# Two row blocks written ahead of their logits, and other warm-up matmuls on TensorE

## The chip, the cores and the metric

The kernel runs on one core of a Trainium2 chip. The metric is the device time of one execution in microseconds (us); the time of a kernel is the median of its runs. TensorE (PE) does matmuls and transposes, VectorE (DVE), ScalarE (ACT) and GpSimd (POOL) do element-wise work, SyncE (SP) issues most DMAs, POOL the indirect ones.

## The reference

Three layers follow one another: attention over 768 positions with a local window and pooled keys, a mixture of 8 experts with a skip score on its output, and a dense layer with a cosine gate.

```python
def _attn_ref(q, k, v):                      # (2, 8, 768, 64)
    k_sum = k.reshape(B, H, nb, 32, D).max(axis=3)
    v_sum = v.reshape(B, H, nb, 32, D).mean(axis=3)
    ...
    a = softmax(concatenate([scores_l_m, scores_s]))
    return a @ concatenate([v, v_sum])

def _moe_ref(x, w_skip, w_gate, w1, w2):     # x (1536, 512)
    do_compute = x @ w_skip > 0
    xc = x[do_compute]
    e_idx = argmax(xc @ w_gate)
    gate_w = softmax(xc @ w_gate)[e_idx]
    for e in range(8):
        h = maximum(xc[e_idx == e] @ w1[e], 0)
        y[e_idx == e] = gate_w * (h @ w2[e])
    out[do_compute] = xc + y

def _moe2_ref(x, w_in, w_out):               # w_in (512, 2048)
    h = x @ w_in
    return (h * cos(h)) @ w_out
```

## The kernel before

The 1536 rows of `x` are 12 blocks of 128. Attention runs as a software pipeline of 24 steps; two steps make one block. A block leaves attention turned (`xT[n]`, features on partitions). `logits` multiplies it with the skip and gate weights (`pl`, eight matmuls in two groups for two blocks, one of four for one), and copies the product out (`ls`). `turn_rows` turns the block back with four transposes into `pk`, from which ACT copies `xtok`, and `write_rows` lets SP write that to `xb` in memory. `st_q` and `st_sum`, together `st_l`, turn the logits (`pq`) and add them up into `LG`. `route1` finds the expert of each row (`R`), `route2` counts places, and `slots` multiplies one-hot matrices (`OR`) with `R` into `pia`, `pib` and `pic`, from which DVE makes the row numbers for the gathers (`GIA` for the first). Blocks 0 to 9 pass through that within the pipeline; blocks 10 and 11 come at its end, and the routing behind them.

POOL gathers the rows of expert 0 and 1 from `xb` by GIA into `xg`; the first needs every row write. When they are there, PE turns them (`ptx`, line 601), multiplies them with the first weights of the expert (`ph`, line 639), then does the second half of `slots` (line 575), the next `ptx` and the next expert. POOL goes on with the gathers of all other experts (`xg`, `xo`, `xm`). Then come the experts, and the dense layer (`pf` line 1219, `py` line 1398) to the end.

Engines run their instructions in the order of the code, each its own queue; the code is that order, with no scheduler behind it. Weights come in pieces from a list: `load_piece(after, lag)` lets SP issue the next piece, behind a given instruction where one is given, else at an ordinary pace.

`warm` (line 166) issues matmuls of zeros whose results nobody reads: 512 columns wide, or narrow with 64. They stand at the beginning (while the first keys load), in attention step 3, between the parts of the routing (`W1_`, `W2_`, `W3_` = 3, 3, 4, all wide) and behind the routing (`WN` = 7 wide and 56 narrow), while the first gather is under way.

```python
W1_, W2_, W3_, WN = 3, 3, 4, 7
```

Of the kernel before, what the change touches and what calls it, by code (L numbers as in the profile page):

```python
# [19 lines left out]
P = 128  # L20
# [10 lines left out]
NT = NTOK // P  # L31
# [9 lines left out]
W1_, W2_, W3_, WN = 3, 3, 4, 7  # L41
# [78 lines left out]
def tile_kernel(ctx: ExitStack, tc: tile.TileContext, consts, qh, kh, vh, vw, w9, w1, w2, w_in, w_out, out):  # L120
    nc = tc.nc
# [8 lines left out]
    xb = dpool.tile([NTOK + 1, DM], F32, name="xb")  # L130
# [34 lines left out]
    def warm(pool, tag, n, w=512):  # L165

        t = pool.tile([P, w], F32, tag=tag, name="warm")
        for _ in range(n):
            nc.tensor.matmul(t, wz[:, 0:P], wz[:, 0:w], start=True, stop=True)
# [8 lines left out]
    def load_w(u):  # L178
        pool = ring[u % NU]
        wt[u] = pool.tile([P, 4096], F32, tag="w", name="w")  # L180
        for part in range(4):
            wq.append((u, part))

    def load_piece(after=None, half=None):

        if not wq:
            return
        u, part = wq.pop(0) if half != 0 else wq[0]
        e, kind = divmod(u, 2)
        k, w = (4, w1) if kind == 0 else (8, w2)  # L190
        ks, fs = slice(part * k // 4, (part + 1) * k // 4), slice(None)
        if half is not None and kind == 0:
            fs = slice(512 * half, 512 * half + 512)
        elif half is not None:
            ks = slice(2 * part + half, 2 * part + half + 1)
        d = nc.sync.dma_start(out=wt[u].rearrange("p (k f) -> p k f", k=k)[:, ks, fs],
                              in_=w[e].rearrange("(k p) f -> p k f", p=P)[:, ks, fs])
        if after is None and len(pieces) >= ahead_of[-1]:
            after = pieces[-ahead_of[-1]]
        if after is not None:  # L200
            tc.add_manual_dep(d.ins, after.ins.name, SYNC, reason="pace")
        pieces.append(d)
# [8 lines left out]
    ps_s = at.enter_context(tc.tile_pool(name="ps_s", bufs=2, space=PSUM))  # L211
    ps_t = at.enter_context(tc.tile_pool(name="ps_t", bufs=2, space=PSUM))
    ps_x = at.enter_context(tc.tile_pool(name="ps_x", bufs=1, space=PSUM))
    ps_m = at.enter_context(tc.tile_pool(name="ps_m", bufs=3, space=PSUM))
# [85 lines left out]
    def kend(b):  # L300
        nc.gpsimd.tensor_copy(out=kT[b][:, :, SK - QT:SK], in_=kT[b][:, :, 0:QT])
# [38 lines left out]
    def st_norm(i, fill=None):  # L340
        sm, su = sc[i]
        nc.vector.tensor_scalar(out=su, in0=su, scalar1=1e-9, scalar2=None, op0=ALU.add)
        if fill is not None:
            fill()
        nc.vector.reciprocal(out=su, in_=su)  # L345
        nc.gpsimd.tensor_tensor(out=sm, in0=sm, in1=su.unsqueeze(2).to_broadcast([P, NP, P]), op=ALU.mult)  # L346
# [30 lines left out]
    xT = {}  # L377
# [36 lines left out]
    rows = {}  # L414
    IOB = ap_.tile([P, NS], BF16, name="IOB")

    def logits(n, eng):

        s = xT[n]
        pl = ps_m.tile([P, P], F32, tag="m", name="pl")  # L420
        for p in range(NP):
            nc.tensor.matmul(pl[32 * p:32 * p + 32, :], w9s[:, p, :], s[:, p, :], start=True, stop=True,
                             skip_group_check=True)
        ls = a2.tile([P, P], F32, tag="ls", name="ls")
        eng(out=ls, in_=pl)
        xT[n] = ls
        return s

    def turn_rows(n, s, pool, tag):
        pk = pool.tile([P, NP, P], F32, tag=tag, name="pk")  # L430
        for p in range(NP):
            nc.tensor.transpose(pk[:, p, :], s[:, p, :], ident)
        rows[n] = a3.tile([P, DM], F32, tag="xtok", name="xtok")
        nc.scalar.copy(out=rows[n], in_=pk.rearrange("p n a -> p (n a)"))

    def write_rows(n):
        nc.sync.dma_start(out=xb[n * P:(n + 1) * P, :], in_=rows.pop(n))

    def st_x(n):
        turn_rows(n, logits(n, nc.vector.tensor_copy), ps_m, "m")  # L440
# [74 lines left out]
    def one_hot(ns, a, b):  # L515
        for n in ns:
            nc.vector.tensor_scalar(out=OR[:, n, a:b], in0=IOB[:, a:b], scalar1=RK[:, n:n + 1],
                                    scalar2=None, op0=ALU.is_equal)
# [156 lines left out]
    kput(0, slice(0, NP), 1, 6, nc.scalar.copy)  # L675
    for u in range(4):
        load_w(u)
    warm(ps_t, "t", 27)
    warm(ps_t, "t", 12, 64)
    for i in range(NI - 1):  # L680
        fill, hot = (), None
        if i >= 8 and i % 2 == 0:
            fill, hot = route1_parts((i - 8) // 2)
        if i >= 10 and i % 2 == 0:
            fill = (lambda f=fill[0], n=(i - 10) // 2: (one_hot((n,), 0, NS), f()),) + fill[1:]
        if i != 4:
            st_scores(i, fill)
        if i == 6:
            kend(0)
        if i == 5:  # L690
            nc.gpsimd.tensor_copy(out=IOB, in_=cst[:, C_IOTA:C_IOTA + NS])
            nc.vector.tensor_copy(out=ub, in_=cst[:, C_U:C_U + P])
            nc.vector.tensor_copy(out=G5[:, :, 0:1], in_=cst[:, C_TT:C_TT + NT].unsqueeze(2))
            nc.vector.tensor_copy(out=G5[:, :, 1:2], in_=cst[:, C_P:C_P + 1].unsqueeze(1).to_broadcast([P, NT, 1]))
        if i >= 1:
            st_norm(i - 1, hot)
        if hot is not None:
            route2_ids((i - 8) // 2)
        if i == 3:
            warm(ps_x, "x", 6)  # L700
        if i >= 3:
            st_T(i - 3)
        if i in (3, 4):
            for j in (range(3), range(3, 6))[i - 3]:
                vmean_mm(0, j)
            if i == 4:
                vmean_copy(0)
                st_scores(i)
        st_exp(i)
        if i in (4, 14):  # L710
            vmean_spread(i // 14)
        if i >= 4:
            st_pv(i - 4)
        if i in (12, 13):
            for j in (range(4), range(4, 6))[i - 12]:
                vmean_mm(1, j)
        if i >= 9 and i % 2 == 1:
            route2_parts((i - 9) // 2)()
        if i >= 6 and i % 2 == 0:
            st_x((i - 6) // 2)  # L720
        if i >= 7 and i % 2 == 1:
            st_q((i - 7) // 2)
        if i in KS:
            kpool(1, KS.index(i))
        if i == 9:
            kpool_out(1, slice(0, NP))
            kput(1, slice(0, NP), 0, 6, nc.vector.tensor_copy)
            kend(1)
        if i == 13:
            vmean_copy(1)  # L730
        if i == NQ + 3:
            early.close()
            lists = ctx.enter_context(tc.tile_pool(name="lists", bufs=1, side="right"))
            GIA, SIA, GIB, SIB, GIS, SIS = (lists.tile([n, NE], U32, name=m) for n, m in (
                (QA, "GIA"), (QA, "SIA"), (P, "GIB"), (P, "SIB"), (YT, "GIS"), (YT, "SIS")))
            GTA, GTB, GTS, SEL = (lists.tile([n, NE], F32, name=m) for n, m in ((QA, "GTA"), (P, "GTB"), (YT, "GTS"), (P, "SEL")))
            wpb = ctx.enter_context(tc.tile_pool(name="wpb", bufs=2, side="right"))
            ring[4] = ring[5] = wpb
            load_w(4)
            load_w(5)  # L740
        if i == 7:
            nc.sync.dma_start(out=xb[NTOK:NTOK + 1, :], in_=wz.bitcast(F32)[0:2, :])
        if PC(i) and i % 2:
            load_piece()
        for _ in range(MORE.get(i, 0)):
            load_piece()
        if i % 4 == 2 and (i + 6) // 2 < NI // 2:
            load_q((i + 6) // 2)
        if i >= 7 and i % 2 == 1:
            write_rows((i - 7) // 2)  # L750

        if i >= 4 and i % 2 == 0 and i != NQ + 2:
            load_v(i - 1)
        if i == NQ:
            load_v(NQ + 1)
        if i % 2 == 0:
            window(i)
        if 2 <= i <= 5:
            load_k(1, i - 2)
        if 5 <= i <= 10:  # L760
            load_vn(1, i - 5)
        if PC(i) and i % 2 == 0:
            load_piece()
# [25 lines left out]
    route2((NT - 4,))  # L789
    last_pv(L)  # L790
    st_l(NT - 3)
    rows11 = logits(NT - 1, nc.vector.tensor_copy)
    rows10 = logits(NT - 2, nc.scalar.copy)
    route1((NT - 3,))
    turn_rows(NT - 1, rows11, ps_x, "x")
    write_rows(NT - 1)
    st_l(NT - 1)
    st_l(NT - 2)
    turn_rows(NT - 2, rows10, ps_m, "m")
    write_rows(NT - 2)  # L800
    load_piece()
    pia = ps_t.tile([QA, 6, NE], F32, tag="t", name="pia")
    pib = ps_t.tile([P, 6, NE], F32, tag="t", name="pib")
    pic = ps_x.tile([YT, 6, NE], F32, tag="x", name="pic")
# [44 lines left out]
    warm(ps_s, "s", W3_)  # L849
    slots(pib, lb, tail)  # L850
    slots(pic, lc, tail)
    warm(ps_s, "s", WN)
    warm(ps_s, "s", 56, 64)
    slot_ids(pib, idb)
    load_piece(slot_gi(idb, False, GIB), 1)
    slot_ids(pic, idc)
# [458 lines left out]
    for e in range(NE):  # L1315
# [18 lines left out]
        if e == 4:  # L1334
            cv_alloc(0, 0)
            t = wpa.tile([P, 2, 4, 512], F32R, tag="w", name="yb")
# [4 lines left out]
        if e == 6:  # L1341
            t = wpb.tile([P, 4096], F32, tag="w", name="y4")
# [188 lines left out]
```

## Time and profile before

| | us |
|---|---|
| median of 3 runs | 479.47 |
| lowest and highest | 478.92, 479.60 |
| the profiled execution | 479.16 |
| its span, first to last instruction | 477.2 |
| PE, PEld, DVE, ACT, POOL busy | 437.9, 319.6, 301.2, 214.2, 142.5 |

PEld is PE's loading of weights, which overlaps its matmuls. Busy shares are over the whole span, while the stages have different limits; so the table by stage and the timeline are to be read with them. "Issue" is time in which an engine waited for nothing that the profile shows, "remote" a wait for a signal whose sender the profile doesn't name. In the timeline a row is a group of like instructions that follow one another: start, length, engine, line, what it writes and reads, count, and in brackets how long the engine was idle before and what ended that.

### The profile page before, as it was taken

The numbers are of one execution on the slowest core, as the hardware profiler recorded it, in microseconds if no ns is written. First come the engines' busy times: TensorE is split into PE (matmuls) and PEld (weight loads), VectorE is DVE, ScalarE is ACT, GpSimd is POOL, SyncE is SP. The second block draws the span as 40 slices with busy tenths as digits, with TensorE's granted clock in tenths as the row PEclk, the third lists the DMA queues.
The fourth block names the chain that finished last, engine by engine and source line by source line (L and its number), as shares of the span: only waits on it lengthen the run. The fifth ranks groups of instructions, "written<-read, shape, count | busy, mean of one in ns | idle before, by whom it ended". The sixth has DMA issues, their size and how long they took to land.

```text
span 477.2 us, 9227 instructions
## 1 busy us (share of the span) xinstructions
PE 437.9 (92%) x3273; PEld 319.6 (67%) x3276; DVE 301.2 (63%) x842; ACT 214.2 (45%) x523; POOL 142.5 (30%) x170
## 2 busy tenths in 40 slices
PE   8899999509989897999999999999999999999994
PEld 4667676304444343567888888888888888888883
DVE  5697897106040051567679797998989956472831
ACT  2988993001332123346567566473646415051600
POOL 0755762650120024454053222231222100003043
PEclk9999999857999999999999999999999999999999
DMA  8999998799958389324312232321322000002021
GB/s 265 322 310 330 346 302 277 233 279 365 384 178 337 131 311 396 90 73 128 117 40 93 89 102 80 129 88 46 100 78 88 0 1 0 1 1 88 2 110 66
DMA packets 35180, 76.05 MB, mean 159 GB/s; under 512 B 4185, under 2 KB 10843, under 8 KB 35124
## 3 DMA queue, kind: packets, MB, share of 16 engines
q1 hardware_dynamic: 31876, 66.07, 42.2%
q0 software_dynamic: 3248, 9.27, 6.1%
q8 instruction: 31, 0.51, 0.5%
q14 instruction: 25, 0.20, 0.1%
HBM read 68.15 MB, written 7.60 MB: 159 GB/s over the span
## 4 chain that ended last, share of the span: by engine, by line
PE 29%; issue 18%; DVE 3%; POOL 3%; POOLq 0%; ACT 0%; DVEq 0%; ACTq 0%
PE pf L1219 14%; PE py L1398 11%; PE py L1464 2%; POOL out L627 2%; DVE g L1235 1%; PE pt L1144 1%; POOL wx L938 1%; DVE cvu L929 0%; DVE cvc L930 0%; DVE u L1225 0%; DVE c L1229 0%; POOLq L1527 0%; DVE nn L1224 0%; DVE cvu L927 0%; ACT u L1223 0%
## 5 line engine op out<-in xcount | busy, mean ns | idle before, releaser
L1219 PE MATMUL pf<-yb,wx 128*128 128x512 f32 x576 | 133.9, 390 | 1.3 <-DVE xg L1006 0.8
L1219 PEld LDWEIGHTS pf<-yb,wx 128*128 128x128 f32 x576 | 107.7, 188 | 24.2 <-PEq L1199 1.3
L1398 PE MATMUL py<-wx,g 128*128 128x512 f32 (+1 forms) x540 | 121.6, 384 | 0.0
L1398 PEld LDWEIGHTS py<-wx,g 128*128 128x128 f32 x540 | 99.9, 188 | 20.2
L1223 ACT ACTIVATE u<-pf,qbias 128x512 f32<-128x512 f32 x44 | 30.1, 685 | 78.2 <-PE pf L1219 78.0
L938 POOL TENSOR_TENSOR wx<-cvc,wx 128x512 fp32r<-128x512 f32 x24 | 34.7, 1446 | 94.7 <-ACT wx L937 91.5
L1404 DVE TENSOR_TENSOR ya<-py,ya 128x512 f32<-128x512 f32 (+1 forms) x37 | 23.8, 672 | 28.2 <-PE py L1398 26.2
L1235 DVE TENSOR_TENSOR g<-c,g 128x512 fp32r<-128x512 f32 x40 | 41.3, 1032 | 0.1
L336 ACT ACTIVATE sm<-sm,nm 128x128 f32<-128x128 f32 x96 | 37.4, 393 | 2.1 <-DVE nm L324 2.0
L1228 ACT ACTIVATE c<-u 128x512 f32<-128x512 f32 x44 | 27.6, 627 | 16.0 <-DVE g L1235 16.0
L627 POOL DMA_INDIRECT out<-ya,PERM x11 | 10.9, 992 | 79.9 <-DVE ya L1404 79.2
L1224 DVE TENSOR_SCALAR nn<-u 128x512 f32<-128x512 f32 x44 | 18.6, 424 | 23.1 <-ACT u L1223 23.0
L1225 DVE TENSOR_TENSOR u<-u,nn 128x512 f32<-128x512 f32 x44 | 30.5, 693 | 1.5
L1229 DVE TENSOR_TENSOR c<-pf,c 128x512 f32<-128x512 f32 x44 | 30.1, 684 | 0.7 <-ACT c L1228 0.7
L346 POOL TENSOR_TENSOR sm<-sm,su 128x512 f32<-128x512 f32 x23 | 24.2, 1050 | 21.3 <-DVE su L345 10.8
L324 DVE CUSTOM_DVE_ANT_0 sm<-sc,cst 128x128 f32<-128x128 f32 x96 | 23.6, 284 | 7.0 <-PE sc L317 6.0
L1234 ACT CAST g<-c 128x512 fp32r<-128x512 f32 x44 | 26.7, 607 | 0.2 <-DVE c L1229 0.2
L937 ACT CAST wx<-cvc 128x512 fp32r<-128x512 f32 x24 | 14.9, 622 | 16.1 <-DVE cvc L930 16.1
L1083 DVE SCALAR_TENSOR_TENSOR xm<-pox,GTB,xm 128x512 f32<-128x512 f32 x2 | 1.5, 750 | 30.4 <-PE pox L1073 30.4
L627 POOL DMA_INDIRECT xb<-xg,SIA x8 | 7.8, 978 | 41.9 <-DVEq L1199 15.5
L317 PE MATMUL sc<-kT,q 64*64 64x128 f32 x384 | 17.5, 282 | 2.3 <-DVE nm L324 1.4
L929 DVE SCALAR_TENSOR_TENSOR cvu<-cvc,cvu 128x512 int32<-128x512 int32 x24 | 17.5, 731 | 3.0 <-DVE cvu L927 0.5
(256 smaller groups left out, 631.5 us busy)
## 6 DMA issues: line engine op xcount, KB each, us to landing
w<-w SPq DMA_DIRECT2D x62, 512.0 KB
raw<-w_in SPq DMA_DIRECT2D x16, 512.0 KB
raw<-w_out SPq DMA_DIRECT2D x16, 512.0 KB
kT<-kh SPq DMA_DIRECT2D x8, 384.0 KB
vn<-vh SPq DMA_DIRECT2D x12, 256.0 KB
xb<-xtok SPq DMA_DIRECT2D x12, 256.0 KB
q<-qh SPq DMA_DIRECT2D x4, 512.0 KB
vt<-vw SPq DMA_DIRECT2D x12, 128.0 KB
```

Of the source, the lines that this page charges most:

```text
L336: nc.scalar.activation(out=sm[:, p, :], in_=sm[:, p, :], func=AF.Exp, scale=-1.0, bias=nm[:, p:p + 1], accum_out=su[:, p:p + 1])
L346: nc.gpsimd.tensor_tensor(out=sm, in0=sm, in1=su.unsqueeze(2).to_broadcast([P, NP, P]), op=ALU.mult)
L627: return nc.gpsimd.indirect_dma_start(out=dst, out_offset=bass.IndirectOffsetOnAxis(ap=idx, axis=0), in_=src, in_offset=None, bounds_check ...
L938: eng.tensor_tensor(out=lo, in0=c, in1=hi.bitcast(F32), op=ALU.subtract)
L1219: nc.tensor.matmul(p, w[:, k, fs], y[:, k, :], start=(n == 0), stop=(n == 11))
L1223: nc.scalar.activation(out=u, in_=p, func=AF.Identity, scale=1.0 / (2.0 * math.pi), bias=qbias)
L1225: nc.vector.tensor_tensor(out=u, in0=u, in1=nn, op=ALU.subtract)
L1228: nc.scalar.activation(out=c, in_=u, func=AF.Sin, scale=TWO_PI)
L1229: nc.vector.tensor_tensor(out=c, in0=p, in1=c, op=ALU.mult)
L1234: nc.scalar.copy(out=gh, in_=g)
L1235: (nc.gpsimd if i in POOL_G else nc.vector).tensor_tensor(out=gl, in0=g, in1=gh.bitcast(F32), op=ALU.subtract)
L1398: nc.tensor.matmul(p, a[:, ws], b[:, f, cs], start=(n == 0), stop=(n == 11))
```

## The change

`logits` can take a block from outside, and `write_rows` returns its DMA. At the end of attention blocks 10 and 11 are turned and written first, and their logits come behind; before, both logits came first, then the rows of block 11, then those of block 10. The weight piece after them is issued behind the write of block 11. Of the warm-ups, 7 of 27 wide ones at the beginning go, and 35 narrow ones join the 12; the 6 wide ones of step 3 become 36 narrow; behind the routing 15 wide ones stand in the place of 7 wide and 56 narrow.

```diff
-    def logits(n, eng):
-
-        s = xT[n]
+    def logits(n, eng, s=None):
+
+        s = xT[n] if s is None else s
...
     def write_rows(n):
-        nc.sync.dma_start(out=xb[n * P:(n + 1) * P, :], in_=rows.pop(n))
+        return nc.sync.dma_start(out=xb[n * P:(n + 1) * P, :], in_=rows.pop(n))
...
-    warm(ps_t, "t", 27)
-    warm(ps_t, "t", 12, 64)
+    warm(ps_t, "t", 20)
+    warm(ps_t, "t", 47, 64)
...
         if i == 3:
-            warm(ps_x, "x", 6)
+            warm(ps_x, "x", 36, 64)
...
     st_l(NT - 3)
-    rows11 = logits(NT - 1, nc.vector.tensor_copy)
-    rows10 = logits(NT - 2, nc.scalar.copy)
+    turn_rows(NT - 2, xT[NT - 2], ps_m, "m")
+    write_rows(NT - 2)
+    turn_rows(NT - 1, xT[NT - 1], ps_x, "x")
+    last_in = write_rows(NT - 1)
+    logits(NT - 1, nc.vector.tensor_copy)
+    logits(NT - 2, nc.scalar.copy)
     route1((NT - 3,))
-    turn_rows(NT - 1, rows11, ps_x, "x")
-    write_rows(NT - 1)
     st_l(NT - 1)
     st_l(NT - 2)
-    turn_rows(NT - 2, rows10, ps_m, "m")
-    write_rows(NT - 2)
-    load_piece()
+    load_piece(last_in)
...
     slots(pib, lb, tail)
     slots(pic, lc, tail)
-    warm(ps_s, "s", WN)
-    warm(ps_s, "s", 56, 64)
+    warm(ps_s, "s", WN + 8)
```

PE at the end of attention, before: `px` is the last attention product, `pq` first of block 9, and the last two rows are the slots of the blocks up to 9.

```order
L386 MATMUL px<-aT,vt_120 64x64 x16
L445 MATMUL pq<-ident,ls 128x128
L422 MATMUL pl<-xT,w9s 32x128 x8
L432 MATMUL pk<-ident,xT 128x128 x4
L445 MATMUL pq<-ident,ls 128x128 x2
L432 MATMUL pk<-ident,xT 128x128 x4
L575 LDWEIGHTS OR
L575 MATMUL pia<-R_77,OR 64x24
```

PE at the same place, after:

```order
L386 MATMUL px<-aT,vt_120 64x64 x16
L445 MATMUL pq<-ident,ls 128x128
L432 MATMUL pk<-ident,xT 128x128 x8
L422 MATMUL pl<-xT,w9s 32x128 x8
L445 MATMUL pq<-ident,ls 128x128 x2
L575 LDWEIGHTS OR
L575 MATMUL pia<-R_77,OR 64x24
```

All eight transposes `pk` now stand ahead of the logits `pl`; before, four stood between `pl` and `pq` and four behind `pq`.

ACT at the end of attention, before: the last copies of attention, and behind them the exponentials of the gates (`r_ex`).

```order
L434 COPY xtok<-pk 128x512
L412 COPY xT<-px 128x256
L425 COPY ls<-pl 128x128
L434 COPY xtok<-pk 128x512 x2
L550 ACTIVATE r_ex<-r_ex 128x96
```

ACT at the same place, after:

```order
L434 COPY xtok<-pk 128x512
L412 COPY xT<-px 128x256
L434 COPY xtok<-pk 128x512 x2
L425 COPY ls<-pl 128x128
L550 ACTIVATE r_ex<-r_ex 128x96
```

The copy of the logits of block 10 now comes behind both copies of rows.

## Rows read from the trace of the kernel before

**Rows 1.** The page's chain that ended last, shares by engine:

```profile
PE 29%; issue 18%; DVE 3%; POOL 3%; POOLq 0%; ACT 0%; DVEq 0%; ACTq 0%
```

**Rows 2.** Table by stretch: its length, each engine's busy time, clock, DMA share, GB/s:

```profile
9.45:75.60 66.15, 62.15 (x1112) 45.33 (x1113) 55.37 (x363) 59.06 (x238) 38.82 (x61) 1.00 1.02 321
75.60:86.00 10.40, 10.05 (x149) 7.00 (x147) 8.53 (x61) 2.09 (x5) 3.21 (x8) 1.00 0.71 255
86.00:89.50 3.50, 2.85 (x51) 1.77 (x51) 0.12 (x1) 0.27 (x1) 2.39 (x3) 1.00 0.69 200
89.50:107.70 18.20, 2.32 (x24) 1.76 (x22) 0.00 (x0) 0.38 (x1) 11.32 (x13) 0.59 1.02 278
...
215.00:477.20 262.20, 254.40 (x1148) 211.12 (x1148) 192.26 (x302) 119.47 (x209) 58.22 (x46) 1.00 0.21 66
```

**Rows 3.** Waits from 86 to 109, total, times, longest:

```profile
DVE s_ii L590 <- remote: 21.8, 1, 21.8
...
ACT cst L642 <- remote: 9.2, 1, 9.2
```

**Rows 4.** Timeline from the first weight piece of the routing to expert 1:

```profile
79.08 6.55 SPq L196 DMA_DIRECT2D w<-w  x5
...
80.83 0.22 DVE L583 TENSOR_SCALAR GIA<-ida,cst 64x8 uint32<-64x8 f32 x1
...
82.27 1.12 POOL L623 DMA_INDIRECT xg<-xb,GIA  x1 [2.12 <-DMA w<-w]
...
82.62 3.32 PE L169 MATMUL warm<-wz 128*128 128x512 bf16 x62
...
85.98 0.30 PE L601 MATMUL ptx<-ident,xg 64*128 64x64 f32 x2
...
86.50 0.91 POOL L623 DMA_INDIRECT xg<-xb,GIA  x1 [1.89 <-PE ptx L601]
...
86.64 1.93 PE L639 MATMUL ph<-w,cst 128*32 128x256 f32 x32 [0.35 <-ACT cst L602]
...
87.79 0.27 SPq L915 DMA_DIRECT2D raw<-w_in  x1
...
103.57 0.91 POOL L623 DMA_INDIRECT xo<-xb,GIS  x1 [0.30 <-issue]
...
107.80 0.39 PE L601 MATMUL ptx<-ident,xg 64*128 64x64 f32 x2 [1.93 <-issue]
...
108.73 3.64 PE L639 MATMUL ph<-w,cst 128*32 128x256 f32 x32
```

**Rows 5.** Warm-ups alone: early wide, later wide, narrow; length, PE busy (count), clock, DMA share, GB/s:

```profile
1.20:4.20 3.00, 2.98 (x8) 1.00 0.64 183
4.30:8.30 4.00, 4.00 (x20) 1.00 1.14 307
84.20:85.70 1.50, 1.50 (x55) 1.00 0.49 175
```

**Rows 6.** Timeline, PE's work behind the warm-ups of the beginning and of step 3:

```profile
9.48 0.33 PEld L317 LDWEIGHTS sc<-kT,q 64*64 64x64 f32 x7 [0.57 <-ACT kT L298]
...
14.35 0.42 PEld L371 LDWEIGHTS pt<-ident,sm 128*128 128x128 f32 x4 [0.36 <-POOL sm L346]
```

**Rows 7.** Timeline: one block's transposes in attention, then the end of attention:

```profile
57.48 0.66 PE L432 MATMUL pk<-ident,xT 128*128 128x128 f32 x4
58.07 0.67 PE L317 MATMUL sc<-kT,q 64*64 64x128 f32 x16
...
75.96 0.54 PEld L422 LDWEIGHTS pl<-xT,w9s 128*32 128x32 f32 x16 [0.23 <-DVE xT L412]
...
76.71 0.66 PE L432 MATMUL pk<-ident,xT 128*128 128x128 f32 x4
...
77.40 1.24 ACT L434 COPY xtok<-pk 128x512 f32<-128x512 f32 x2 [0.31 <-PE pk L432]
...
78.01 0.97 SPq L437 DMA_DIRECT2D xb<-xtok  x2
```

## The prediction

> **What bounds the kernel now.** I read the page's chain of waits first, then a table of the whole span by stage, then the timeline of the stages that the diff names. The chain [rows 1] goes back through TensorE (PE) work and through "issue" time, in which an engine waited for nothing that the profile shows. The table [rows 2] says where PE is not the bound: in the last 262.20 us it is busy 254.40, and in attention 62.15 of 66.15. The exception is 89.50 to 107.70, where PE works 2.32 us of 18.20, DVE nothing, and where the clock falls (0.59 granted, against 1.00 in the stages before). The reader is to see there a stretch in which engines stand although the code has work for them.
>
> The waits of that stretch [rows 3] say what kind of stretch it is. ACT waits 9.2 us for the result of `ph`, and DVE 21.8 us for `pia`, both put down to "remote". The timeline [rows 4] puts it in place: `ph` runs 86.64 to 88.57, yet PE only gets to the second `ptx` at 107.80, with 1.93 us of "issue" ahead of it. The frame around it is POOL's train of gathers: the first `xg` goes at 82.27, and from 86.50 (released by `ptx`) 15 follow one another until the last at 103.57 for 0.91, so one every 1.22 us. So I take this as the limit of the middle of the program: while POOL issues its train, signals and PE's instructions come through late, and about 3.3 us after its end (104.48 to 107.80) they flow again. What the change is worth is read from **when that train starts and how long the limp lasts**; what comes after is PE back to back and shifts with it.
>
> **The change part by part.**
>
> *Warm-ups at the beginning.* 27 wide and 12 narrow become 20 and 47: 7 wide go, 35 narrow come. A wide one costs about 0.375 us in the first 3 us (8 in 3.00) and 0.20 after that (20 in 4.00), a narrow one 0.027 (55 in 1.50) [rows 5]. The slow first ones all stay, so the part is 7 x 0.20 = 1.40 less and 35 x 0.027 = 0.95 more: PE is done 0.45 us earlier. It hides: the first scores load at 9.48 after 0.57 us of waiting for ACT's `kT`, and no PE order moves that [rows 6]. Cost 0. With the gap grown from 0.57 to about 1.0, the clock could fall; that is a rival below.
>
> *Attention step 3.* 6 wide (1.20 by the same rate) become 36 narrow (0.98). PE waits there for POOL's `sm` until 14.35 [rows 6], so again 0, with 0.2 us more of idle.
>
> *Row blocks 10 and 11 ahead of their logits.* On PE eight transposes now stand before the eight pairs of `pl`. Four take 0.59 us from their start to that of the next work (57.48 to 58.07) [rows 7], so eight 1.18. Before, `pl` started at 75.96 after 0.23 us of waiting for `xT`; the transposes of block 10 need no such wait, so they take that 0.23 away: `pl` starts 1.18 - 0.23 = **0.95 later**, at 76.91. What hangs on `pl`: `ls` on DVE, then `route1` of block 9, which is queued behind that copy on DVE, then the logits' sums, `route1` of blocks 10 and 11, the slot numbers and GIA, which ends at 81.05 [rows 4]: now 82.00. On ACT `ls` of block 10 comes behind the two `xtok` copies. These start 0.69 after the transposes before (76.71 to 77.40), so at 76.42, and with 1.24 for both end at 77.66, while `pl` of block 10, the second half of a group that took 0.54 to load, is done near 77.5: at most 0.2 of further delay on that one copy, which DVE's work for block 9 covers.
>
> The row writes go the other way. They went at 78.01 when the copies were done, 0.97 for both [rows 7]; the copies are done 0.98 earlier, so both go near 77.0 to 77.7. The first gather needs both GIA and the last row write. It started at 82.27, 1.22 after GIA; the profile puts that on the landing of a DMA (it names `w`, the gather reads `xb`) [rows 4]. So before, the writes ended last. After, they land 0.98 earlier (81.3 at the latest), and GIA ends at 82.00: **the ids take the place of the row write**, and the gather goes at 82.00 plus the step from DVE to POOL. That step is not shown by itself; it lies between 0 and 1.22, so the gather between 82.00 and 83.22. I take 0.2, since POOL follows the end of `ptx` by 0.22 (85.98 + 0.30 to 86.50) [rows 4], so 82.2: no gain, since what one side gives the other takes.
>
> `load_piece(last_in)`: the five pieces of `w` that went from 79.08 over 6.55 us of SP's queue now wait for the last row write to land, until between 79.1 and 81.3. Behind it on SP stand these pieces, then a weight raw at 87.79, 2.16 us after the end of those pieces [rows 4]. The delay of up to 2.2 us fits that gap, and the DMA engines have room (0.71 and 0.69 busy in the two stages [rows 2]). Cost 0; without that cover, up to 2.2.
>
> *Warm-ups behind the routing.* 7 wide and 56 narrow took 3.32 from 82.62 to 85.94, where `ptx` starts without a gap [rows 4]. 15 wide are 8 x 0.20 = 1.60 more and 56 x 0.027 = 1.51 less [rows 5]: 0.1 longer. But they start behind `slots` of the last blocks, which hang on `R`: 0.95 later, and end near 86.9. Before, `ptx` found its gathered rows at about the time when the warm-ups ended; after, the rows are there (gather unchanged) and the warm-ups are late. How far `ptx` waited for the warm-ups and how far for its rows, the trace doesn't split within a tenth or two; so of 0.95 + 0.1 I keep 0.86, `ptx` near 86.84 for 85.98, and with it `ph` and POOL's train, which `ptx` releases: **+0.86**. The limp then has the same 15 gathers to wait through and keeps its length.
>
> *The sum.* 0 + 0 + 0 + 0.86 on the profiled execution's 479.16 (span 477.2) is 480.0. That execution lies 0.3 below the median 479.47, so on the median **480.3**. Bounds: without any delay of `ptx` 479.5; with the gather's 1.22 kept behind GIA, `xg` comes 0.95 later and so does `ptx`: 480.5; with 0.1 of rounding at both ends the case spans 479.9 to 480.7.
>
> **Rivals.**
>
> *Fewer instructions ahead of the train (faster).* Behind the routing 48 matmuls with 48 weight loads disappear, and the removed ones were the densest stretch of PE's program: 55 in 1.50 us. If what chokes in the limp is a store of records or signals that PE fills and POOL's train keeps from emptying, a shorter queue lets PE run on before it stalls. Before, PE did the `ph` of expert 0 and part of `slots`, and some 20 matmuls of `pib` and `pic` were left in the limp (24 of all kinds touch it [rows 2]); 48 more would bring it through these, `ptx`, `pth` and most of the next `ph`, which took 3.64 us at 108.73 [rows 4]. That is 3.64 plus about 0.7 off, less the 0.86 above: 3 to 4 us, **476**, with 474 to 478 as its span. For it: the late signals of `ph` and `pia` [rows 3]. Against: POOL answers `ptx` 0.22 after its end, so no signal was held up yet when the train began. [...]
>
> *The limp goes altogether (faster).* If the narrow warm-ups are its cause, up to the 15.9 us in which PE does nothing come back. But the DMA engines are at 1.02 of their time there [rows 2], so much of it turns into waiting for weights or gathered rows: I price it at half, 8, up to 14: **471**, 465 to 472. Against: the limp outlasts the warm-ups by 20 us and ends with the train.
>
> *The clock falls in attention (slower).* The narrow matmuls leave PE idle 0.45 us more at 9.48 and 0.2 more at 14.35. If the clock goes to half there, each us of PE work costs another: `ph` took 3.64 at the low clock and 1.93 at the high one [rows 4], and the clock averages 0.59 over 18.20 us here [rows 2]. In attention 5 to 8 us of work at half clock make **484 to 487**. It decides from the moment when the table shows less than 1.00 before 75. Against: gaps of 0.5 us pass without that [rows 2, 6].
>
> *It does nothing at all.* If `pl` is not later, because the transposes find room in the wait for `xT`, or the gather still waits for something else: **479.5**.
>
> **How the numbers follow.** Forecast (+0.4 to +1.2) 0.50; fewer instructions 0.22; limp gone 0.06; nothing 0.10; slower by more (clock 0.06, weights late or a longer limp 0.06) 0.12. Predicted is the forecast, 480.3. The range leaves out the limp's end, the clock and a little of the 476 case: 474.5 to 482.0. A measurement of this kernel can tell about 0.2%, 0.96 us, from no change. The forecast lies at 0.8, so of its 0.50 I put 0.28 within and 0.22 beyond; with 0.10 for nothing same is 0.36 less 0.02 for its slower edge; slower 0.22 + 0.12 + 0.02; faster 0.22 + 0.06 = 0.28, and 0.02 for a gather that does gain comes from same: faster 0.30, same 0.34, slower 0.36.
>
> **What would show it.** Right: `pl` near 76.9, GIA ending near 82.0, the first gather at 82.1 to 82.4 put down to DVE, `ptx` at 86.7 to 86.9 directly behind the warm-ups, the train from 87.3, the second `ptx` near 108.6 and the same table from there. A second `ptx` before 106, or `ph` of expert 1 run before the train ends, shows the first rival; a granted clock under 1.00 before 90 the third. The forecast is wrong if the time from the train's start (86.50) to the second `ptx` (107.80) is not 21.3 us within 0.5.

## The result, and the profile after

The changed kernel takes 483.3 us (482.07 to 483.77) where the kernel before takes 479.47, a ratio of 1.0081 with an interval of 1.0067 to 1.0095: 3.8 us slower, where 480.3 and at most 482.0 were forecast. Its profiled execution has a span of 481.6, 4.4 more than before.

The table by stretch of the changed kernel, columns as in [rows 2]:

```profile
9.45:75.60 66.15, 62.31 (x1143) 45.96 (x1143) 55.37 (x363) 59.01 (x238) 38.77 (x61) 1.00 1.00 316
...
86.00:89.50 3.50, 1.23 (x10) 0.48 (x12) 0.65 (x5) 0.27 (x1) 1.80 (x2) 0.97 0.74 219
89.50:107.70 18.20, 6.30 (x63) 3.05 (x57) 0.00 (x0) 0.00 (x0) 11.85 (x13) 0.59 0.96 239
...
116.00:215.00 99.00, 88.34 (x670) 43.05 (x671) 32.02 (x68) 29.23 (x61) 25.62 (x30) 0.98 0.69 252
```

The limp is still there (89.50 to 107.70, clock 0.59). New are 86.00 to 89.50, where PE has 1.23 us of work for 2.85, and 116 to 215, in which the prediction saw no change: 88.34 at a clock of 0.98, where the table of the kernel before has

```profile
116.00:215.00 99.00, 90.26 (x682) 45.46 (x674) 34.64 (x69) 29.80 (x63) 28.13 (x34) 1.00 0.67 242
```

The timeline of the changed kernel at the places of [rows 4]:

```profile
76.84 0.38 PEld L422 LDWEIGHTS pl<-xT,w9s 128*32 128x32 f32 x16 [0.17 <-issue]
...
81.52 0.22 DVE L583 TENSOR_SCALAR GIA<-ida,cst 64x8 uint32<-64x8 f32 x1
...
81.81 4.49 SPq L196 DMA_DIRECT2D w<-w  x5
...
82.65 1.12 POOL L623 DMA_INDIRECT xg<-xb,GIA  x1 [1.78 <-DVE r_sm L553]
...
83.30 3.41 PE L169 MATMUL warm<-wz 128*128 128x512 bf16 x15
...
86.63 0.17 DVE L585 TENSOR_SCALAR GIS<-idc 64x8 uint32<-64x8 f32 x1
87.18 0.90 POOL L623 DMA_INDIRECT xg<-xb,GIA  x1 [2.19 <-DMA w<-w]
...
88.62 0.33 PE L601 MATMUL ptx<-ident,xg 64*128 64x64 f32 x2 [1.91 <-DMA xg<-xb,GIA]
...
89.31 3.58 PE L639 MATMUL ph<-w,cst 128*32 128x256 f32 x32 [0.35 <-issue]
...
108.63 0.47 PE L601 MATMUL ptx<-ident,xg 64*128 64x64 f32 x2
...
110.15 3.40 PE L639 MATMUL ph<-w,cst 128*32 128x256 f32 x32 [0.42 <-ACT cst L602]
```

GIA ends at 81.74, 0.69 later than before, and POOL's train starts at 87.18, 0.68 later. But the first gather now takes until 88.62 to bring its rows; `ptx` waits 1.91 for them, and `ph` runs at a low clock (0.53 granted from 89.3 to 92.9): 3.58 for the 1.93 of before. The `ph` of expert 1, behind the limp, is 1.42 later than before (110.15 for 108.73). The other 3 us come later, at two places where PE waits for "issue" in the middle of a product. The first is in the changed kernel alone. Up to there the delay has shrunk to 0.76 (118.47 for 117.71). Before, the 32 matmuls of that `po` run through:

```profile
117.71 1.93 PE L998 MATMUL po<-w,hT 128*32 128x256 f32 x32
```

After:

```profile
118.47 1.70 PE L997 MATMUL po<-w,hT 128*32 128x256 f32 x25
120.75 0.64 PE L997 MATMUL po<-w,hT 128*32 128x256 f32 x7 [0.58 <-issue]
```

The second is in both. Before:

```profile
177.66 1.06 PE L1144 MATMUL pt<-ident,xo 128*128 128x128 f32 x8 [0.33 <-PEq L1199]
178.56 0.38 PE L986 MATMUL pth<-ident,h 128*128 128x128 f32 x2
178.87 1.93 PE L639 MATMUL ph<-w,xe 128*32 128x256 f32 x32
180.74 0.33 PE L601 MATMUL ptx<-ident,xg 64*128 64x64 f32 x2
181.00 0.62 PE L998 MATMUL po<-w,hT 128*32 128x256 f32 x3
182.58 1.92 PE L998 MATMUL po<-w,hT 128*32 128x256 f32 x29 [0.96 <-issue]
184.43 0.46 PE L1014 MATMUL ptx<-ident,xo 64*128 64x64 f32 x4
```

After:

```profile
179.24 1.06 PE L1143 MATMUL pt<-ident,xo 128*128 128x128 f32 x8 [0.33 <-PEq L1198]
180.14 0.38 PE L985 MATMUL pth<-ident,h 128*128 128x128 f32 x2
180.45 1.93 PE L639 MATMUL ph<-w,xe 128*32 128x256 f32 x30
184.21 0.59 PE L639 MATMUL ph<-w,xe 128*32 128x256 f32 x2 [1.83 <-issue]
184.73 0.40 PE L601 MATMUL ptx<-ident,xg 64*128 64x64 f32 x2
185.65 3.20 PE L997 MATMUL po<-w,hT 128*32 128x256 f32 x32 [0.52 <-ACT h L642]
188.79 0.46 PE L1013 MATMUL ptx<-ident,xo 64*128 64x64 f32 x4
```

From `pth` on the changed kernel was 1.58 later (180.14 for 178.56); at the `ptx` behind `po` it is 4.36 later (188.79 for 184.43). Before, PE stood in `po`, three matmuls in; after, two matmuls before the end of `ph`, so that ACT got `ph` late, PE waited another 0.52 for ACT, and `po` took 3.20 for about 1.9, at a low clock (0.72 granted from 184 to 190, where the kernel before has 1.00). That is 2.78 of the 4.4 at one place where the code is the same in both kernels.

### The profile page after: what moved, and what is told of

It is laid out like the page before. It is cut to its first block, busy times and chain, and to the rows that moved or that the text cites. A ratio compares the mean times of both kernels' runs of the same rounds, so it can differ in the third digit from the quotient of the medians.

```text
span 481.6 us, 9250 instructions
## 1 busy us (share of the span) xinstructions
PE 441.2 (92%) x3286; PEld 320.3 (66%) x3286; DVE 301.1 (63%) x842; ACT 213.8 (44%) x523; POOL 142.6 (30%) x170
## 4 chain that ended last, share of the span: by engine, by line
PE 29%; issue 18%; DVE 3%; POOL 3%; POOLq 0%; ACT 0%; DVEq 0%; ACTq 0%
PE pf L1218 14%; PE py L1397 11%; PE py L1463 2%; POOL out L627 2%; DVE g L1234 1%; PE pt L1143 1%; POOL wx L937 1%; DVE cvu L928 0%; DVE cvc L929 0%; DVE u L1224 0%; DVE c L1228 0%; POOLq L1526 0%; DVE nn L1223 0%; DVE cvu L926 0%; ACT u L1222 0%
```

## The experiments

The question is why. Theory P: PE stops where its next instructions have not arrived (the expectations call it a stand), and that place is counted in instructions from the start; the change has 35 - 7 + 30 - 48 = 10 matmuls more ahead of later code, so the stop comes ten matmuls earlier in the program. Rival T: it is the routing's delay and the cold `ph`, and the later stops follow from other times.

PE's matmuls and loaded weights from the start of the span into the second stop, the sixth and eighth columns of the table by stretch; before, and after:

```profile
0.00:181.70 181.70, 154.60 (x1900) 91.54 (x1904) 92.58 (x513) 82.28 (x292) 67.51 (x105) 0.94 0.89 293
```

```profile
0.00:182.20 182.20, 155.51 (x1906) 91.38 (x1907) 92.78 (x513) 81.32 (x289) 67.36 (x105) 0.94 0.89 290
```

1900 and 1906: about the same count, though it is another instruction; records that a trace can miss (that of before has 115 of the 118 warm-up matmuls of the code, the other all 128), weights that are loaded ahead (1904 and 1907 of them here) and instructions that the profile doesn't count lie between the two. The DMA view has the same story: in both kernels the page counts 31 pieces of 0.51 MB together on an instruction queue (q8), so about 16 KB each, and one of them starts shortly ahead of each stop. The DMA queues of the kernel before from 180.1 to 180.3, then of the changed one from 181.5 to 181.7 (packets, MB, share of 16 engines):

```profile
q1 hardware_dynamic: 18, 0.06, 78.6%
q8 instruction: 1, 0.02, 34.2%
```

```profile
q8 instruction: 1, 0.02, 34.2%
q1 hardware_dynamic: 7, 0.02, 31.9%
```

PE goes on 2.4 and 2.6 us after the start of that piece, and is read here as waiting for it both times; what differs is what it could do meanwhile. In all fourteen profiles of this case PE's next matmul behind this stop (in e4, behind its stop in `ph`) comes 2.35 to 2.58 us after the start of such a piece. The profile doesn't say whose instructions a piece holds: that they are PE's is read from this order. Not every piece stops PE like that: in the last 262.20 us of the kernel before nine of them come, and PE is busy 254.40; at these two stops it stands 0.96 and 1.83. Both start behind a jump (the `If` at the end of an expert's code, `PEq` in the rows of `pt` above): 4.0 us behind that `pt` before, 3.1 after. That the jump is the reason was not tried.

The runs came on two sorts of chips. On that of e5 to e8 the kernel before takes 479.25, and the kernels profiled there limp as above (in e8 PE works 3.10 us from 89.50 to 107.70). On those of e1 to e4 and e9 to e12 it takes 461.6 and 461.1, and the kernels profiled there don't limp (shown at e10); there single executions spread by 2 to 4 us to either side. So ratios are to the kernel before on the same chip; they are not the quotient of the two medians, which can differ from them by up to 0.2%.

**e1, e5, e6: the changed kernel, and with ten narrow warm-ups fewer.**

```diff
-    warm(ps_t, "t", 47, 64)
+    warm(ps_t, "t", 37, 64)
```

> The changed kernel with 37 narrow warm-ups at the beginning in the place of 47, so that from the routing's end on PE has as many instructions behind it as in the kernel before. Theory P (place in PE's code): the changed kernel's loss is 1.0 us from the routing and the rest, some 3.5 us in its profile, from PE standing for new instructions at 182.4 to 184.2 in the last two matmuls of a `ph`, ten matmuls earlier than the stand of 0.96 us before; with ten matmuls fewer the stand returns into `po`, the clock dip at 184.9 goes, and the time is 480.2 to 480.9. Rival T (it is the later start of POOL's train and the cold `ph` that do it, wherever the code lies): 483.3, as ten narrow matmuls in the shade of the first loads are worth nothing.

> The changed kernel itself, beside the kernel before on the same chip as the next three. Where the stretch behind the routing shows the limp: 1.008 of the kernel before. Where the chip lets PE run on there (as in the runs of e1 to e4): theory P, the 1.0043 of e1 plus the 10 matmuls that cost e2 0.9%, so 1.010 to 1.014, with a stand of 2 to 2.6 us two matmuls before the end of a `ph`. Rival T (it is the routing alone): as e1, 1.004.

> The changed kernel with 37 narrow warm-ups at the beginning again, now beside the changed kernel itself. Theory P: 0.5 to 1.0% faster than e5, the stand back in `po`. Rival T: equal to e5 within 0.3%.

e1: 463.95, 1.0043 (1.0005 to 1.0081), between what the two theories gave, on a chip where the changed kernel itself was not run. Where PE doesn't limp, the two parts of e1 cost nothing that can be told by themselves (e3 and e10 below), so where its 0.4% comes from stays open. On the chip that limps e5, the changed kernel, takes 483.56, 1.0087 (1.0063 to 1.0111), and e6 with ten matmuls fewer 480.17, **1.0013** (0.9997 to 1.0028). Ten matmuls of zeros at the beginning, which nobody waits for, are worth 3.4 of the 4.3 us. In e6 the stop is back in `po`, at the old count, and the first stop is gone; the timeline, and the count into the stop:

```profile
119.27 1.93 PE L997 MATMUL po<-w,hT 128*32 128x256 f32 x32
...
183.90 1.92 PE L997 MATMUL po<-w,hT 128*32 128x256 f32 x29 [0.64 <-issue]
```

```profile
0.00:183.30 183.30, 155.88 (x1901) 91.63 (x1904) 92.73 (x513) 82.24 (x292) 67.37 (x105) 0.94 0.88 291
```

The profiled execution of e5 has the stop in `ph` (1.55 of issue) but no low clock behind it (1.00 from 178 to 200, where the changed kernel's profile shows 0.92). Its span is 479.6, 2 us under the other, and its time 481.67, while most of e5's are 483.3 to 484.5. From the `pt` ahead of the stop to the `pth` that starts at 199.86 in the kernel before, that kernel takes 22.20 us and e5 23.44; the changed kernel's profile takes 25.12, and that of e7, with a stop of 1.57 and a low clock behind it, 25.10. So the stop at its new place costs 1.2 us more than at the old one, the low clock that can follow it another 1.7, and the first stop (0.57 in e5) about what is left of the 3.4.

**e2, e9: the kernel before with ten more.**

```diff
-    warm(ps_t, "t", 12, 64)
+    warm(ps_t, "t", 22, 64)
```

> The kernel before with 22 narrow warm-ups at the beginning in the place of 12, and nothing else: PE's later instructions lie ten matmuls further on, as in the changed kernel. Theory P: the stand moves from `po` into the last matmuls of `ph`, the clock dips behind it, 482 to 483.2. Rival T: 0.29 us more of warm-ups in 0.57 us of waiting, 479.5.

> The kernel before with 22 narrow warm-ups at the beginning in the place of 12, as e2, for a run beside the next three. In all kernels so far PE stopped for instructions behind 1900 to 1906 matmuls, whatever these were. Theory P: the stop comes two matmuls before the end of `ph`, 482 to 483.2 where the kernel before takes 479.3 and PE limps behind the routing, a ratio of 1.006 to 1.009; where it doesn't limp, 1.009 as in e2. Rival T (nothing but the routing costs): 1.000.

466.36, 1.0087 (1.0048 to 1.0126), and 464.99, 1.0084 (1.0041 to 1.0126). These ten alone put both stops where the changed kernel has them and cost as much as the whole change (1.0087 in e5), with the old row blocks and the old warm-ups behind the routing. On these chips the first stop is there without them too, behind two of the `ptx` that follow that `po` (1.18 in e10, 1.47 in e11); the second grows from 1.23 and 1.49 there to 1.85. The stops in e9, and the count into the second:

```profile
101.53 0.64 PE L998 MATMUL po<-w,hT 128*32 128x256 f32 x7 [1.26 <-issue]
```

```profile
163.65 0.59 PE L639 MATMUL ph<-w,xe 128*32 128x256 f32 x2 [1.85 <-issue]
```

```profile
0.00:163.00 163.00, 150.36 (x1903) 89.71 (x1907) 92.25 (x513) 81.69 (x289) 67.62 (x105) 1.00 0.99 326
```

The time is some 20 us earlier than in the changed kernel, the instruction the same, the count the same: the stop is tied to the count and not to the time. T falls as the account of these stops.

**e3, e11: the row blocks alone.** The kernel before with this part of the change and nothing else:

```diff
-    rows11 = logits(NT - 1, nc.vector.tensor_copy)
-    rows10 = logits(NT - 2, nc.scalar.copy)
+    turn_rows(NT - 2, xT[NT - 2], ps_m, "m")
...
-    load_piece()
+    load_piece(last_in)
```

> The kernel before with the part on the row blocks alone (turned and written ahead, the weight piece behind the last write); all warm-ups as before, so PE's code keeps its places. Theory P: the routing's 0.7 us and a late, cold first `ph`, +0.8 to +1.3, 480.3 to 480.8, with the stand in `po`. Rival T: most of the 3.8, 482.5 to 483.3.

> The kernel before with the row blocks alone, as e3, beside e10. Theory P with the prediction's own sum: POOL's train starts 0.6 to 0.9 later and the rest with it, 480.0 to 480.5, ratio 1.001 to 1.0025 where PE limps, 1.000 where it doesn't (e3). If the later weight pieces cost by themselves: up to 481.

461.92, 1.0001 (0.9972 to 1.0029), and 462.07, 1.0014 (0.9975 to 1.0054): no difference that can be told on these chips. What the part costs on a chip that limps is bounded by e6 alone.

**e10: the warm-ups alone, with the place kept.** All warm-ups of the change, but 37 for 47:

```diff
-    warm(ps_t, "t", 27)
-    warm(ps_t, "t", 12, 64)
+    warm(ps_t, "t", 20)
+    warm(ps_t, "t", 37, 64)
...
-            warm(ps_x, "x", 6)
+            warm(ps_x, "x", 36, 64)
...
-    warm(ps_s, "s", WN)
-    warm(ps_s, "s", 56, 64)
+    warm(ps_s, "s", WN + 8)
```

> The kernel before with all the warm-ups of the change (beginning, step 3, behind the routing), but 37 narrow ones at the beginning in the place of 47, so that later code keeps its place; the row blocks as before. If the warm-ups cost nothing by themselves: 479.0 to 479.8, ratio 0.999 to 1.001, and the 0.1% of e6 belongs to the row blocks. If fewer records behind the routing help (the prediction's first rival): PE gets further within the limp, and the time falls by 3 us. If fewer narrow ones behind the routing or more idle cost clock: over 480.5.

461.21, 1.0002 (0.9966 to 1.0037): where they stand the warm-ups cost nothing, as forecast. That chip shows no limp, so the first rival was not tried by it. The stretch of [rows 2] in e10, where PE works 16.16 of 18.20 us beside the same train of POOL:

```profile
89.50:107.70 18.20, 16.16 (x179) 8.34 (x177) 9.18 (x49) 3.20 (x10) 11.50 (x13) 0.91 1.03 271
```

**e4, e8, e12: other places.** Fewer matmuls ahead of later code: by 48 (15 wide behind the routing for 7 and 56), by 12 (none of the narrow ones at the beginning), by 24:

```diff
-    warm(ps_s, "s", WN)
-    warm(ps_s, "s", 56, 64)
+    warm(ps_s, "s", WN + 4)
+    warm(ps_s, "s", 28, 64)
```

> The kernel before with 15 wide warm-ups behind the routing in the place of 7 wide and 56 narrow, and nothing else: 48 matmuls fewer ahead of all later code. The prediction's first rival (fewer instructions ahead of the gathers let PE run on before it limps): 475 to 477, with the second `ptx` before 106. Theory P: the limp stays, its end at 107.8 within 0.3, and the time changes only by where the stand for instructions comes to lie, 48 matmuls later: 478.5 to 479.7. Rival T: 479.5.

> The kernel before without the 12 narrow warm-ups at the beginning: PE's later code 12 matmuls nearer to the start. Theory P: the stand for instructions moves 12 matmuls on in the program, from the third to the fifteenth of the 32 matmuls of a `po`, and shrinks by what 12 of them take (0.7 us) to 0.2 to 0.3, if no other place gets worse: 478.6 to 479.0 where the kernel before takes 479.5, a ratio of 0.998 to 0.999. Rival T: 1.000, since 0.35 us of warm-ups is not missed at the beginning.

> The kernel before with 11 wide and 28 narrow warm-ups behind the routing in the place of 7 and 56: 24 matmuls fewer ahead of later code, the same time (4 x 0.20 more, 28 x 0.027 less). Theory P: the stop behind 1900 to 1906 matmuls comes to lie in the last five matmuls of `po`, when the new instructions have arrived, so it goes: 0.5 to 0.96 us off, 478.5 to 479.0, ratio 0.998 to 0.999; a new stop elsewhere takes it back. Rival T: 1.000.

e4: 469.64, **1.0175** (1.0133 to 1.0218, four executions), far outside of all that was expected. e8: 479.03, 0.9995 (0.9976 to 1.0015); e12: 461.47, 0.9997 (0.9960 to 1.0033); neither shows the gain. The places came out as P gives them. Before, 29 matmuls of `po` are left behind the stop; in e8, with 12 fewer ahead, 17, and the stop is 0.49:

```profile
183.21 1.24 PE L997 MATMUL po<-w,hT 128*32 128x256 f32 x17 [0.49 <-issue]
```

In e12, with 24 fewer, 5 are left, and the stop shrank to 0.19; but a jump far ahead of it got long (it takes 0.71 in e10). The two places:

```profile
98.22 0.66 PE L986 MATMUL pth<-ident,h 128*128 128x128 f32 x2 [3.23 <-PEq L1199]
```

```profile
166.42 0.63 PE L998 MATMUL po<-w,hT 128*32 128x256 f32 x5 [0.19 <-issue]
```

e4 has the same at that jump and more behind it:

```profile
99.43 0.66 PE L985 MATMUL pth<-ident,h 128*128 128x128 f32 x2 [4.31 <-PEq L1198]
```

```profile
162.28 2.80 PE L639 MATMUL ph<-w,xe 128*32 128x256 f32 x28 [3.08 <-issue]
...
170.19 1.94 PE L1143 MATMUL pt<-ident,xo 128*128 128x128 f32 x8 [2.30 <-PEq L1198]
```

Its stop in `ph` comes behind 1746 matmuls and not 1900, against what is expected at e9 of all kernels: which counts PE stops at changes with the code, and why e4 loses so much more stays open. So moving the code moves every stop at once; in e12 the jump takes 2.5 us more than in e10, where the first stop, now gone, took 1.18 and the second, now 0.19, 1.23; and in e8 the 0.47 us that the stop shrank are less than the interval can tell. None of the three beats the kernel before.

**e7: the weight pieces at their ordinary pace.**

```diff
-    load_piece(last_in)
+    load_piece()
```

> The changed kernel with the weight pieces at their ordinary pace in the place of behind the last row write. If the pieces that stand behind the write, and so just ahead of the first gather in the DMA queues, are what brings `xg` late: `xg` lands 1.0 to 2.4 us earlier, `ptx` goes behind the warm-ups without a gap, and the time falls by 0.5 to 1.5 us from e5. If the row write's own landing decides: `ptx` and the time as in e5 within 0.5 us. PE's places in the code are as in e5, so the stand in `ph` stays.

482.44, 1.0060 (1.0036 to 1.0084), 1.1 under e5, with intervals that overlap. The trace shows the expected: the first gather goes at 82.78 and `ptx` follows the warm-ups at 87.04, where in e5 it waited until 88.70. What it gains is little; the rows speak for a limp that ends with POOL's train:

```profile
82.78 1.12 POOL L623 DMA_INDIRECT xg<-xb,GIA  x1 [1.52 <-DMA w<-w]
...
87.04 0.33 PE L601 MATMUL ptx<-ident,xg 64*128 64x64 f32 x2
87.72 0.90 POOL L623 DMA_INDIRECT xg<-xb,GIA  x1 [2.60 <-PE ptx L601]
```

```profile
103.41 0.26 PE L601 MATMUL ptx<-ident,xg 64*128 64x64 f32 x1 [2.65 <-issue]
...
109.73 0.65 PE L639 MATMUL ph<-w,cst 128*32 128x256 f32 x4 [0.31 <-ACT cst L602]
```

PE is at the second `ptx` by 103.41, earlier than the 107.80 of [rows 4]. Still the `ph` of expert 1 starts at 109.73, 22.0 us after the train's start, as before (86.50 to 108.73, 22.2): PE got further, and the copy of ACT between them came only at 109.41, behind the train's end. This speaks against the price of the prediction's first rival, whose gain was that PE runs on ahead of its signals.

## Why the prediction was wrong

**The step that failed is the warm-ups' cost of zero.** Each of the three parts was priced where it stands, and there the price was right (e10, 1.0002, on a chip where PE doesn't limp). What was left out is the sum that the prediction had all the terms of: 10 more matmuls and weight loads ahead of everything behind the routing. The reader of [rows 2] was told that what comes after the limp is PE back to back and shifts with it. It is not: the stop of 0.96 us in `po` at 182.58 stood in the trace of the kernel before, and it hangs on the count of instructions ahead. This term, put at nothing, measured 3.4 us (e5 against e6); with it the forecast's 0.86 would have been 4.3, what e5 shows.

**The rest of the sum held by its size, not by its steps.** e6 is the changed kernel without that term: 0.9 over the kernel before by the medians (480.17 for 479.25, interval -0.1 to 1.3), for 0.86 forecast. That the two meet is in part luck, since most steps to it came out otherwise. `pl` starts at 76.84 for 76.91 and GIA ends at 81.74 for 82.00, so the delay there is 0.69 and not 0.95. The row writes did go 1 us earlier (until 77.93 for 78.98), but the gather went at 82.65, later than the 82.1 to 82.4 that was given. `ptx` came at 88.62, where 86.84 was forecast. That `ptx` releases POOL's train is wrong: in the changed kernel the train starts at 87.18, ahead of `ptx` at 88.62. In both kernels it starts 0.38 after GIS, DVE's last slot numbers, ends (86.12 to 86.50, and 86.80 to 87.18), and in all fourteen profiles 0.38 to 0.57 after it; the row of before:

```profile
85.95 0.17 DVE L585 TENSOR_SCALAR GIS<-idc 64x8 uint32<-64x8 f32 x1
```

By that the delay reaches the train by DVE and not by the warm-ups; it was not tried.

**`load_piece(last_in)` at zero was wrong in kind.** The pieces did go into the gap on SP, but they were 0.84 us ahead of the first gather in place of 3.2, and it took longer behind them: 5.97 from its start to `ptx` (82.65 to 88.62) for 3.7 before and 4.26 in e7 (82.78 to 87.04). e7 takes that away and gains 1.1, not clear of its interval. The bound of 2.2 that was set beside it covers it.

**The rivals.** The limp stayed, so the second fell. Of the third, the clock: its sign, less than 1.00 before 90, did show (0.97 from 86 to 89.50), but behind the wait of `ptx`; in attention, where the rival has it, the clock stays 1.00, and the fall that cost time came behind the stop at 184. The first rival's sign, a second `ptx` before 106, did not show in the changed kernel (108.63), though it has the 48 matmuls fewer; in e7, where PE was ahead (103.41), the next `ph` came behind the end of the train all the same. The store of records or signals that this rival supposes is shown by no trace or run of this case. The check set beside the forecast, 21.3 us from the train to the second `ptx`, came out at 21.45 (87.18 to 108.63).

## What to carry to other kernels

Count the instructions that an edit adds ahead of later code, here on PE, also where they cost nothing: a stop in the middle of like matmuls with "issue" ahead of it hung on that count, and ten matmuls more moved it to a place where another engine waits for it, which cost 3.4 us (e5 against e6). Before a small change is judged, compare it with padding that keeps the count; here that turned a loss of 0.87% into one of 0.13%. The stop that moved began 4.0 us behind a jump before and 3.1 after, and the DMA engines' share was 1.04 from 178 to 184 in both kernels.

## What the runs showed of the hardware that was not expected

- From the start of a piece of instructions of about 16 KB (0.51 MB in 31) to PE's next matmul behind the stop it took 2.4 to 2.6 us (180.1 to 180.3 until 182.58, and 181.5 to 181.7 until 184.21), with other DMA queues busy (q1 with 78.6% and 31.9%). The transfer of the piece itself took 1.09 of that in both (34.2% of what 16 engines have in 0.2 us); what fills the rest is not shown.
- The limp is not the kernel's alone: on some chips PE works 16.16 of the 18.20 us beside the same train of gathers (e10), and the kernel before takes 461.1 and 461.6 us for 479.25. Why chips differ there stays open.
- A stop of PE can be followed by a fall of its clock or not: behind a stop of 1.55 us (e5) the granted clock stays 1.00 from 184 to 190, behind one of 1.57 (e7) and one of 1.83 (the changed kernel's profile) it is 0.72. The fall is worth about 1.7 us here.
